# Four or five magnitude products in the windows of steps 8, 16 and 24, and row results in used-up input rows

## The chip, the cores and the metric

The kernel runs on one core of a Trainium2 chip, alone. The metric is the device time of one execution in microseconds (us). TensorE (PE) multiplies matrices, VectorE (DVE) and ScalarE (ACT) work element by element, GpSimd (POOL) does so too, and SyncE (SP) issues nearly all transfers. Each engine takes its instructions in the order in which they were written and waits where a result or a buffer is missing. SP's queue is such an order as well: a transfer that has to wait keeps back every transfer behind it.

## The reference

Two blocks follow each other, on 2048 tokens (L) of 448 channels (D), in float32:

```
mod = silu(c) @ w_mod                                   # six rows: sa, ca, ga, sb, cb, gb
h = layernorm(x) * (1 + ca) + sa
# S4D: K[d, l] = 2 Re sum_n C[d,n] dt[d] exp(A[d,n] dt[d] l), n = 256; A = -exp(log_A_real) + i A_imag
y = irfft(rfft(h, 2L) * rfft(K, 2L))[:L] + h * D_skip   # a causal convolution along the tokens
x = x + ga * y
h = layernorm(x) * (1 + cb) + sb
x = x + gb * (W2 gelu(W1 layernorm(h)^T + b1) + b2)^T   # an MLP across the tokens, 1792 wide
```

## The kernel before

The change touches only the first third, in which the convolution's kernel K is made while the input's own transform is worked off beside it.

K is made in 56 steps (`NHALF`), each for 16 of the 448 channels and half of the 256 n. A step s needs magnitudes and phases. The magnitudes of eight steps (`BATCH`) are made together in a **window** ahead of the steps 0, 8, 16, 24 and so on, because ACT must change its function table between the exponential and the sine. The eight steps behind a window are called its **set**. In a window, place e (0 to 7) takes on ACT the two exponentials of step s + e into a tile `mag` (`st_exp`), while PE makes the exponents of the next step (`st_exponents`). In a step (`st_step`) ACT takes absolute values and sines of the phases that PE made (`st_phase`, in PSUM), POOL multiplies them with the magnitudes to G (two instructions, L737 and L738), DVE to E (four instructions, L739, L740, L742 and L743), and two steps later PE multiplies G and E into kg (`st_kgen`).

Two of the four E instructions need a second magnitude, m2. It is made on POOL by `st_mag2`: a small product w (L712) and a product m of 128x512 (L717). This pair is called a magnitude product here. In the sets of steps 8, 16 and 24, the products of the first two steps are made in the window (e < 2), and that of step s + 2 during step s for the other six. The m2 tiles come from a ring of three (`m2`), the E tiles from a ring of three (`gp_`, tag E).

Beside it run two other lines of work, spread over windows and steps by hand:

- **Rows.** `u_rows(n)`, n from 0 to 31, multiplies a row block of the input `xt` with a table on PE, and DVE scales the result into a tile (L595). Two n make a pair; a pair's result goes to `yu_d` in DRAM from SP. Pair p reads input row block p of the sixteen in `xt`. Its result tile is one of a ring of three (`yt`), except for the pairs 2 to 4, which borrow two E tiles (`yE`). Once steps 12, 13 and 14 are reached, three loads of `w_mod` (L341) overwrite row blocks 0 to 3, 4 to 7 and 8 to 11 of `xt`, to be read by `modulation` in the window of step 16.
- **Columns.** `u_cols(p)` loads `yi` back from `yu_d` (SP, L617), multiplies on PE (`pu`, L627) and adds on DVE (`uo`, L631). The first loads stand in SP's queue behind the window of step 16; the columns fill the steps from 17 on and the window of step 24.
- **Parameter chains.** `chain(q)` prepares, on DVE, the parameters of the next 128 channels; `more` draws some instructions of it at each place. In the windows, its results (A, s, ph, p, xa) are split on POOL into a high and a low part (`hl`: a CAST, L404, and a subtraction, L406) and stored to `pars` in DRAM by SP (L410). Phases (`lph`) and exponents (`lex`) are loaded from there.

All four compute engines have their order written out by hand (a manual schedule); from step 8 on a scheduler orders SP's queue.

Of the kernel before, what the change touches and what calls it, by code (L numbers as in the profile page):

```python
# [11 lines left out]
F32 = mybir.dt.float32  # L12
# [9 lines left out]
L, D, N, F = 2048, 448, 256, 1792  # L22
P = 128
# [3 lines left out]
NI, NJ = 32, 64  # L27
GD = 16
NG = D // GD
NHALF = 2 * NG  # L30
BATCH = 8
# [201 lines left out]
def tile_adaln_s4d_mixer(ctx, tc, i, out):  # L233
# [19 lines left out]
    with ExitStack() as es:  # L253
# [22 lines left out]
        xp = spec.enter_context(tc.tile_pool(name="xp", bufs=1))  # L276
# [28 lines left out]
        xt = xp.tile([P, 16, D], F32, name="xt")  # L305
# [204 lines left out]
        def angle():  # L510

            for a, s, u, xa, ya in tmp.values():
                S.activation(xa, ya, AF.Arctan)
# [52 lines left out]
            T.matmul(pm, wu, means, start=True, stop=True)  # L566
            dve.append(lambda: V.tensor_copy(means, pm))

        yts, wurs, lent = {}, {}, []

        def u_table(R):
            wurs[R] = xp.tile([P, 2, P], F32, tag="wur", name="wur", bufs=3)
# [3 lines left out]
        def u_rows(n):  # L576

            R, g = divmod(n, 4)
            gp, gl = divmod(g, 2)
            if gl == 0:  # L580
                pair = n // 2
                if pair in (2, 4):
                    E = gp_.tile([P, 2, GD, NJ], F32, tag="E", name="yE")
                    rooms = E.rearrange("p a g j -> p (a g j)")[:, 0 : 4 * D].rearrange("p (h g d) -> p h g d", h=2, g=2)
                    lent.extend(rooms[:, h] for h in range(2))
                yts[R, gp] = lent[pair - 2] if 2 <= pair < 5 else xp.tile([P, 2, D], F32, tag="yt", name="yt", bufs=3)
            if g == 0 and R < 6:
                u_table(R + 2)
            pm = pms.tile([P, D], F32, tag="ms", name="pu")
            p = slice(64 * gl, 64 * gl + 64)  # L590
            T.matmul(pm, wurs[R][p, gp], xt[p, 2 * R + gp], start=True, stop=True)  # L591

            def out():
                mean = means[:, gl, 2 * R + gp : 2 * R + gp + 1]
                stt(yts[R, gp][:, gl], pm, mean, mod[1], ALU.add, ALU.mult)  # L595
                if gl:
                    nc.sync.dma_start(
                        yu_d[:, :, :, R, 2 * gp : 2 * gp + 2].rearrange("o k c g d -> (o k c) (g d)"),
                        yts.pop((R, gp)).rearrange("p g d -> p (g d)"),
                    )  # L600

            dve.append(out)
# [36 lines left out]
                u_load(p + 4)  # L639


        mags, m2s, eg, phs = {}, {}, {}, {}
        v32 = lambda t: t.rearrange("p (d i) -> p d i", i=32)

        def rows_of(g, exps):
# [63 lines left out]
        def st_mag2(s):  # L709
            me = v32(mags[s][:, 0])  # L710
            w = wp.tile([P, GD], F32, tag="w", name="w")
            G.tensor_tensor(w[:, :, None], me[:, :, 31:32], me[:, :, 1:2], ALU.mult)  # L712
            if s in (3, 4, 5):
                m2 = v32(wm0.rearrange("p k d -> p (k d)")[:, -512 * (s - 2) :][:, 0:512])
            else:
                m2 = m2p[s >= 32 and s % BATCH > 2].tile([P, GD, 32], F32, tag="m2", name="m2")
            G.tensor_tensor(m2, me, w[:, :, None].to_broadcast([P, GD, 32]), ALU.mult)  # L717
            m2s[s] = m2

        def st_step(s, between):  # L720
            me, mg_, m2 = v32(mags[s][:, 0]), v32(mags[s][:, 1]), m2s.pop(s)
            E = gp_.tile([P, 2, GD, NJ], F32, tag="E", name="E")
            Gt = gp_.tile([P, 2, GD, NI], F32, tag="G", name="G")
# [15 lines left out]
            V.tensor_tensor(E[:, 1, :, 32:64], m2, se, ALU.mult)  # L739
            V.scalar_tensor_tensor(E[:, 1, :, 31::-1], me[:, :, 31::-1], -1.0, se, ALU.mult, ALU.mult)  # L740
            between()
# [350 lines left out]
        def window(s):  # L1092
            if s:
                aside.append(True)
            angle()
            logs(s == 8)
            if s == 8:
                more(10)
                u_scale()
                u_table(0)  # L1100
                u_table(1)

            if s == 0:
                st_exponents(s)
            for e in range(BATCH):
                st_exp(s + e)

                if e + 1 < BATCH:
                    st_exponents(s + e + 1)
                else:  # L1110
                    st_phase(s)
                mellow()
                flush(dve)
                flush(act)
                if s == 8 and e == 0:
                    tt(mod[1], mod[1], mod[2], ALU.mult)
                if s < 32:
                    more(WPACE[s // 8][e])
                if s == 0 and e >= 4:
                    u_stats(e - 4)  # L1120
                if s == 8 and e in (3, 4):
                    modulation(0, e - 3)
                if s == 8 and e == 5:

                    G.tensor_tensor(mod[0], mod[0], mod[2], ALU.mult)
                if s and e < (2 if s <= 32 else 1):
                    st_kgen(s - (2 if s <= 32 else 1) + e)
                elif e == 5 and s < 24:
                    if s == 8:
                        yks[0] = y0.tile([P, 32, DC], F32, tag="yk", name="yk0")  # L1130
                    st_s1(act)

                for k, e0 in ((4, 1), (5, 3), (3, 6)) if s == 16 else ():
                    if e in (e0, e0 + 1):
                        modulation(k, e - e0)

                if s == 8 and e == 0:
                    warm(7)
                if s == 8 and e == 1:
                    u_means()  # L1140
                if s in (8, 16):
                    some(u_rows, rows, ((0, 2, 2, 2, 2, 0, 2, 2) if s == 8 else (2, 2, 2, 2, 2, 0, 1, 1))[e])
                elif s == 24 and e in (0, 2, 4, 6, 7):
                    some(u_cols, cols, 1)

                if s == 0 and e > 1:
                    st_mag2(e - 2)
                elif s and (e < 2 or s >= 32):
                    st_mag2(s + e)
                if s == 0 and e == 3:  # L1150
                    for r in range(4):
                        dsk_copy(r)
            aside.clear()
            if s == 8:
                flush(dve)
            if s >= 24 and st_s1(dve):
                flush(dve)
            if s == 0:

                S.activation(one, one, AF.Sin)  # L1160

        WPACE = [[0, 2, 2, 1, 1, 1, 1, 1], [2, 2, 2, 2, 1, 3, 3, 1], [4] * 7 + [9], [4] * 8]
        pace = [2] * 5 + [3, 4, 4] + [2] * 24
        for s in range(NHALF):
# [13 lines left out]
            if s % BATCH == 0:  # L1180
                (late_window if s > 32 else window)(s)
                if s == 0:
                    gp_ = right("gp", 3)
# [45 lines left out]
                idle(10)  # L1229
            held = s > 32 and s % BATCH == BATCH - 2  # L1230
            free = s > 7 and not st_s1(hold if held and s + 2 < NHALF else dve if s % BATCH == BATCH - 1 else act)
            if s + 2 < 32 and (s + 2) % BATCH > 1 and s + 2 > 5:
                st_mag2(s + 2)

            if 3 < s < 8:
# [146 lines left out]
    with ExitStack() as es:  # L1382
# [169 lines left out]
        for t in range(16):  # L1552
            ss = slice(t * P, (t + 1) * P)
            xt = ru.tile([P, D], F32, tag="x2", name="x2")
# [42 lines left out]
```

## Time and profile before

| | |
|---|---|
| times of the runs shown | 663.41 us median of 3 (663.27 to 668.56) |
| the profiled execution | 663.85 us |
| its span | 662.1 us |
| granted TensorE clock, mean | 0.984 |
| busy: PE, DVE, ACT, POOL | 612.3, 443.0, 439.9, 269.5 us |
| E on DVE, one of four (L740) | 680 ns, 56 times |
| G on POOL, one of two (L737) | 1283 ns, 56 times |
| m on POOL (L717) | 1053 ns, 53 times |
| column result on DVE (L631) | 672 ns, 32 times |
| windows of steps 8, 16, 24 in the span | about 61 to 79, 112 to 131, 161 to 175 us |

A row of a timeline reads: start, duration, engine, line, operation, out<-in, shapes, count; in brackets the idle time of the engine before it and what ended that. SPq is the time in which SP issues a transfer, PEld a weight load of PE. A row of the chain of waits has start, duration and what. In the table of windows, each engine has its busy time in the stretch and the number of instructions.

### The profile page before, as it was taken

What the parts mean: (1) busy time and instruction counts of PE and PEld (TensorE: products, weight loads), DVE (VectorE), ACT (ScalarE), POOL (GpSimd) and SP (SyncE); (2) the same over time, 40 slices, a digit from 0 to 9 for tenths busy, and PEclk for the clock granted to TensorE, in tenths of its full rate; (3) what the DMA queues carried; (4) which work ended last, traced back from release to release, by engine and by line L of the source; (5) the groups of instructions that cost most, each with busy time, mean ns of one, the idle gap of its engine ahead of it and who ended that gap; (6) DMA issues with size and microseconds to landing.
All of it is one profiled execution on the core that took longest, in us unless ns stands there. A gap on an engine that the chain in (4) does not pass through costs nothing.

```text
span 662.1 us, 19161 instructions
## 1 busy us (share of the span) xinstructions
PE 612.3 (92%) x7639; PEld 442.9 (67%) x7639; DVE 443.0 (67%) x853; ACT 439.9 (66%) x828; POOL 269.5 (41%) x351
## 2 busy tenths in 40 slices
PE   1878998999999999999888999999999999999997
PEld 0444555445455565656544577788999999999996
DVE  8989889689894887868655688777422553333331
ACT  5978888899989999999587678885222522222220
POOL 7785597588599788787563000000000000000000
PEclk9998999989999999999999899999999999999999
DMA  6595747598775557576787999946755275555530
GB/s 145 156 219 166 253 143 257 182 248 268 218 247 178 103 166 218 169 215 182 234 274 227 257 247 234 233 112 196 201 160 153 57 209 164 162 160 166 161 106 28
DMA packets 97858, 123.67 MB, mean 187 GB/s; under 512 B 13717, under 2 KB 79801, under 8 KB 97769
## 3 DMA queue, kind: packets, MB, share of 16 engines
q1 hardware_dynamic: 97032, 120.02, 64.2%
q0 software_dynamic: 736, 2.43, 1.5%
q8 instruction: 60, 0.98, 0.7%
q14 instruction: 30, 0.24, 0.1%
HBM read 88.33 MB, written 33.59 MB: 184 GB/s over the span
## 4 chain that ended last, share of the span: by engine, by line
PE 63%; DMA 11%; DVE 9%; ACT 7%; POOL 4%; issue 4%; SPq 3%; ACTq 0%; DVEq 0%; POOLq 0%
PE o L1563 7%; PE o L1565 7%; PE o L1564 7%; PE acc L1400 6%; PE acc L1401 6%; PE acc L1402 6%; PE xe L667 6%; PE kg L764 6%; DMA w<-in_B_w_dram 3%; PE xg L667 3%; DMA xt<-in_A_u_dram 3%; DMA v_d<-vt 3%; PE pu L591 2%; PE vv L895 2%; PE kx L872 2%
## 5 line engine op out<-in xcount | busy, mean ns | idle before, releaser
L218 ACT CAST whi<-w 128x896 fp32r<-128x896 f32 x64 | 59.7, 939 | 138.5 <-PE o L1564 82.7
L227 DVE TENSOR_TENSOR wlo<-w,whi 128x896 fp32r<-128x896 f32 x64 | 68.1, 1086 | 41.4 <-ACT whi L218 35.1
L737 POOL TENSOR_TENSOR G<-mag,gs 128x512 f32<-128x512 f32 x56 | 71.9, 1283 | 36.4 <-ACT gs L733 36.4
L1400 PE MATMUL acc<-h3h,whi 128*128 128x448 f32 x224 | 83.0, 371 | 1.7 <-ACT h3h L1467 0.9
L1401 PE MATMUL acc<-h3l,whi 128*128 128x448 f32 x224 | 81.4, 363 | 0.5 <-DVE h3l L1474 0.3
L1563 PE MATMUL o<-uh,whi 128*128 128x448 f32 x224 | 81.3, 363 | 0.0
L1565 PE MATMUL o<-uh,wlo 128*128 128x448 f32 x224 | 81.2, 362 | 0.0
L1402 PE MATMUL acc<-h3h,wlo 128*128 128x448 f32 x224 | 81.0, 361 | 0.0
L1564 PE MATMUL o<-ul,whi 128*128 128x448 f32 x224 | 80.6, 360 | 0.0
L764 PEld LDWEIGHTS kg<-E,G 128*32 128x32 f32 x3584 | 56.2, 114 | 33.1 <-issue 18.4
L738 POOL TENSOR_TENSOR G<-mag,gs 128x512 f32<-128x512 f32 x56 | 71.9, 1285 | 0.0
L764 PE MATMUL kg<-E,G 128*32 128x64 f32 x3584 | 65.9, 227 | 6.4 <-issue 4.2
L667 PE MATMUL xg<-tab,lph 64*128 64x512 f32 x112 | 62.0, 553 | 6.6 <-DVE E L743 4.3
L1568 DVE TENSOR_TENSOR y<-o,x 128x448 f32<-128x448 f32 x16 | 10.0, 624 | 79.0 <-PE o L1565 79.0
L667 PE MATMUL xe<-tab,lph 64*128 64x512 f32 x112 | 61.9, 553 | 0.3 <-issue 0.2
L717 POOL TENSOR_TENSOR m<-mag,w 128x512 f32<-128x512 f32 x53 | 55.8, 1053 | 4.2
L1400 PEld LDWEIGHTS acc<-h3h,whi 128*128 128x128 f32 x224 | 42.0, 188 | 14.8 <-issue 2.1
L729 ACT ACTIVATE ab<-xe 128x512 f32<-128x512 f32 x56 | 33.9, 604 | 16.3 <-PE xg L667 9.1
L1401 PEld LDWEIGHTS acc<-h3l,whi 128*128 128x128 f32 x224 | 42.0, 187 | 3.8 <-DVE h3l L1474 0.9
L1565 PEld LDWEIGHTS o<-uh,wlo 128*128 128x128 f32 x224 | 42.1, 188 | 3.4
L1402 PEld LDWEIGHTS acc<-h3h,wlo 128*128 128x128 f32 x224 | 42.0, 187 | 3.1
L1564 PEld LDWEIGHTS o<-ul,whi 128*128 128x128 f32 x224 | 41.9, 187 | 3.0
(257 smaller groups left out, 1399.1 us busy)
## 6 DMA issues: line engine op xcount, KB each, us to landing
w<-in_B_w_dram SPq DMA_DIRECT2D x64, 224.0 KB
w<-in_B_w_dram SPq DMA_DIRECT2D x32, 448.0 KB
yi<-yu_d SPq DMA_DIRECT2D x32, 224.0 KB
us_d<-uo SPq DMA_DIRECT2D x16, 448.0 KB
u<-us_d SPq DMA_DIRECT2D x64, 112.0 KB
v_d<-vt SPq DMA_DIRECT2D x32, 224.0 KB
vt<-v_d SPq DMA_DIRECT2D x14, 448.0 KB
yu_d<-yt SPq DMA_DIRECT2D x13, 448.0 KB
```

What stands on the lines that cost most here:

```text
L218: self.nc.scalar.copy(hi, w)
L227: eng.tensor_tensor(lo, w, hi.bitcast(F32), ALU.subtract)
L667: T.matmul(out[k], lhs[r], rhs[r], start=start, stop=stop)
L737: G.tensor_tensor(Gt[:, 1], mg_, v32(sg), ALU.mult)
L738: G.tensor_tensor(Gt[:, 0], mg_, v32(cg_), ALU.mult)
L764: T.matmul(kg[32 * q : 32 * q + 32, m], Gt[:, c, d], E[:, c, d], start=h == 0 and c == 0 and m == 0, stop=h == 1 and c == 1, skip_group_ch ...
L1400: nc.tensor.matmul(acc[f], hi[:, fs], h3h[:, r], start=r == 0, stop=False)
L1401: nc.tensor.matmul(acc[f], hi[:, fs], h3l[:, r], start=False, stop=False)
L1402: nc.tensor.matmul(acc[f], lo[:, fs], h3h[:, r], start=False, stop=r == 15)
L1563: nc.tensor.matmul(o, hi[:, ks], uh[kh][:, k], start=kh == 0 and k == 0, stop=False)
L1564: nc.tensor.matmul(o, hi[:, ks], ul[kh][:, k], start=False, stop=False)
L1565: nc.tensor.matmul(o, lo[:, ks], uh[kh][:, k], start=False, stop=kh == 1 and k == 6)
```

## The change

Three things are changed together.

1. **More products in the windows.** A table `MSET` says how many of a set's magnitude products are made in its window: four for the set of step 8, five for those of steps 16 and 24, where there were two. In the steps two, three and three products are left out, those of the first steps of a set.
2. **Two of them in a tile of E.** At the start of these windows a tile is taken from the E ring (`mE`); its two halves hold the products of the first two steps of the set. The others take the m2 ring as before.
3. **Row results in used-up input rows.** The pairs 2 to 4 no longer borrow E tiles. The pairs 3, 4, 6, 8 and 14 write their results over row blocks of `xt` that were already read (0 and 1, 2 and 3, 4 and 5, 6 and 7, 12 and 13). The other eleven pairs use the `yt` ring.

```diff
-        yts, wurs, lent = {}, {}, []
+        yts, wurs = {}, {}
+        spare = {3: 0, 4: 1, 6: 2, 8: 3, 14: 6}
...
             if gl == 0:
                 pair = n // 2
-                if pair in (2, 4):
-                    E = gp_.tile([P, 2, GD, NJ], F32, tag="E", name="yE")
...
-                yts[R, gp] = lent[pair - 2] if 2 <= pair < 5 else xp.tile([P, 2, D], F32, tag="yt", name="yt", bufs=3)
+                if pair in spare:
+                    yts[R, gp] = xt[:, 2 * spare[pair] : 2 * spare[pair] + 2]
+                else:
+                    yts[R, gp] = xp.tile([P, 2, D], F32, tag="yt", name="yt", bufs=3)
...
-            if s in (3, 4, 5):
+            if s in rooms:
+                m2 = rooms.pop(s)
+            elif s in (3, 4, 5):
...
         def window(s):
...
+            if s in (8, 16, 24):
+
+                E = gp_.tile([P, 2, GD, NJ], F32, tag="E", name="mE")
+                for k in range(2):
+                    rooms[s + k] = E[:, k].rearrange("p g j -> p (g j)")[:, 0:512].rearrange("p (d i) -> p d i", i=32)
...
-                elif s and (e < 2 or s >= 32):
+                elif s and e < (BATCH if s >= 32 else MSET[s // BATCH]):
                     st_mag2(s + e)
...
+        MSET = [0, 4, 5, 5]
...
-            if s + 2 < 32 and (s + 2) % BATCH > 1 and s + 2 > 5:
+            if s + 2 < 32 and (s + 2) % BATCH >= max(2, MSET[s // BATCH]) and s + 2 > 5:
                 st_mag2(s + 2)
```

The order of the instructions on PE and ACT is the same as before. On POOL, in the window of step 16 (the splits of ph, p and xa, the addition ks), before:

```order
L404 CAST hl<-ph 128x256
L784 TENSOR_TENSOR ks<-ks,dsk 128x8
L406 TENSOR_TENSOR hl<-ph,hl 128x256
L404 CAST hl<-p_1199 128x256
L406 TENSOR_TENSOR hl<-p_1199,hl 128x256
L404 CAST hl<-xa 128x256
L406 TENSOR_TENSOR hl<-xa,hl 128x256
```

and now:

```order
L404 CAST hl<-ph 128x256
L712 TENSOR_TENSOR w<-mag 128x16
L719 TENSOR_TENSOR m_2048<-mag,w 128x512
L786 TENSOR_TENSOR ks<-ks,dsk 128x8
L406 TENSOR_TENSOR hl<-ph,hl 128x256
L404 CAST hl<-p_1206 128x256
L712 TENSOR_TENSOR w<-mag 128x16
L719 TENSOR_TENSOR m_2075<-mag,w 128x512
L406 TENSOR_TENSOR hl<-p_1206,hl 128x256
L712 TENSOR_TENSOR w<-mag 128x16
L719 TENSOR_TENSOR m_2094<-mag,w 128x512
L404 CAST hl<-xa 128x256
```

The products of the steps 18, 19 and 20 stand among the splits now; they stood behind the G of the steps 16, 17 and 18.

On SP, in the steps from 11 on (yu_d: a pair's result; xt<-in_w_mod: a w_mod load; lph: phase parameters), before, from the result of pair 6 on:

```order
L597 DMA yu_d<-yt 128x896
L653 DMA lph_141<-pars_58 32x256
L657 DMA lph_141<-pars_58 64x1x256
L341 DMA xt<-in_w_mod_dram 112x4x448
L597 DMA yu_d<-yt 128x896 x2
L653 DMA lph_139<-pars_58 32x256
L657 DMA lph_139<-pars_58 64x1x256
L597 DMA yu_d<-yt 128x896 x2
L341 DMA xt<-in_w_mod_dram 112x4x448
```

and now, from the same pair on:

```order
L597 DMA yu_d<-xt 128x896
L653 DMA lph_141<-pars_58 32x256
L657 DMA lph_141<-pars_58 64x1x256
L597 DMA yu_d<-yt 128x896
L597 DMA yu_d<-xt 128x896
L653 DMA lph_139<-pars_58 32x256
L657 DMA lph_139<-pars_58 64x1x256
L341 DMA xt<-in_w_mod_dram 112x4x448
L597 DMA yu_d<-yt 128x896 x2
L341 DMA xt<-in_w_mod_dram 112x4x448
```

The second w_mod load has moved from ahead of the results of pairs 7 and 8 to behind them, ahead of those of pairs 9 and 10. The first one, not shown, has moved from between the results of pairs 2 and 3 to behind that of pair 5.

More of the change, by code (lines that the diff above doesn't have):

```diff
@@ L581, in u_rows @@
                 pair = n // 2
-                if pair in (2, 4):
-                    E = gp_.tile([P, 2, GD, NJ], F32, tag="E", name="yE")
-                    rooms = E.rearrange("p a g j -> p (a g j)")[:, 0 : 4 * D].rearrange("p (h g d) -> p h g d", h=2, g=2)
-                    lent.extend(rooms[:, h] for h in range(2))
-                yts[R, gp] = lent[pair - 2] if 2 <= pair < 5 else xp.tile([P, 2, D], F32, tag="yt", name="yt", bufs=3)
+                if pair in spare:
+                    yts[R, gp] = xt[:, 2 * spare[pair] : 2 * spare[pair] + 2]
+                else:
+                    yts[R, gp] = xp.tile([P, 2, D], F32, tag="yt", name="yt", bufs=3)
             if g == 0 and R < 6:
@@ L639, in u_cols @@
                 u_load(p + 4)
-        mags, m2s, eg, phs = {}, {}, {}, {}
+        mags, m2s, eg, phs, rooms = {}, {}, {}, {}, {}
         v32 = lambda t: t.rearrange("p (d i) -> p d i", i=32)
```

## The prediction

> **What bounds the kernel now.** The page's list of waits says little about the sets of eight steps, so I read first the chain of waits from 175 to 206 us, which covers the third of the three changed sets (its `by line` sum), and beside it the busy time of each engine in the stretches where the steps run.
>
> ```profile
> by line: POOL G L737 28.8%; POOL G L738 24.1%; issue 17.7%; DMA pars<-hl 9.8%; POOL m L717 5.2%; ACT L696 4.1%; POOL w L712 3.9%; ACT gs L734 2.0%; ACT mag L696 1.9%; ACT xg L735 1.6%; POOL hl L406 1.5%; ACT ks L778 1.0%; POOL hl L404 0.9%;
> ...
> core 0: us, PE busy (x) PEld busy (x) DVE busy (x) ACT busy (x) POOL busy (x), PEclk, DMA share, GB/s
> 144.97:162.90 17.93, 17.70 (x412) 9.63 (x401) 17.93 (x30) 16.81 (x36) 17.31 (x18) 1.00 0.89 272
> 179.00:201.60 22.60, 21.68 (x483) 11.71 (x475) 22.60 (x39) 20.28 (x41) 22.13 (x25) 1.00 0.78 248
> ```
>
> The chain runs through POOL: G and the products m fill it. Taken alone it says that a product less on POOL is a product less in time. The windows below it speak against that: DVE is busy for 17.93 of 17.93 us and for 22.60 of 22.60 us in the second and third set, POOL for 17.31 and 22.13. Both are full. So the next question is what a product costs, and where POOL really keeps somebody waiting.
>
> ```profile
> 97.58 0.26 POOL L712 TENSOR_TENSOR w<-mag 128x16 f32<-128x16 f32 x1
> 97.91 1.05 POOL L717 TENSOR_TENSOR m<-mag,w 128x512 f32<-128x512 f32 x1
> 98.92 1.28 POOL L737 TENSOR_TENSOR G<-mag,gs 128x512 f32<-128x512 f32 x1
> ...
> 201.17 1.29 POOL L737 TENSOR_TENSOR G<-mag,gs 128x512 f32<-128x512 f32 x1
> ...
> 201.36 0.61 ACT L732 ACTIVATE xe<-xe 128x512 f32<-128x512 f32 x1
> 202.49 0.60 ACT L733 ACTIVATE gs<-xg 128x512 f32<-128x512 f32 x1 [0.52 <-POOL G L737]
> ```
>
> A product is its w and its m: from 97.58 to 98.92, so 1.34 us of POOL. The one place where ACT waits for POOL in the third set is step 31: L733 starts at 202.49 when G of step 30 ends (201.17 and 1.29 is 202.46), 0.52 us late. In the steps before it, ACT follows PE and DVE; POOL merely falls behind, and nobody needs its G until two steps later. The second set has no such wait.
>
> In the first set DVE stops once:
>
> ```profile
> 96.04 0.37 SPq L341 DMA_DIRECT2D xt<-in_w_mod_dram  x1
> ...
> 102.15 0.67 DVE L595 SCALAR_TENSOR_TENSOR yt<-pu,means,mod 128x448 f32<-128x448 f32 x1
> 104.32 0.68 DVE L595 SCALAR_TENSOR_TENSOR yt<-pu,means,mod 128x448 f32<-128x448 f32 x1 [1.50 <-DMA yu_d<-yt]
> ...
> 96.50 7.72 DMA yu_d<-yt
> ```
>
> DVE waits 1.50 us, to 104.32, for a buffer of the result ring yt, whose transfer (issued 96.50) took 7.72 us behind a w_mod load issued at 96.04 on the same queue.
>
> **The change, part by part.** All durations are of the profiled execution, which took 663.85 us (span 662.1); the median of the runs shown is 663.41, so 0.44 is taken off at the end. Differences are written with a sign, plus being slower.
>
> *Products out of the steps (2, 3 and 3 of them).* POOL is relieved of 2.7, 4.0 and 4.0 us. DVE, full in sets two and three, keeps the pace: two E products, two more and two uo, as before. What remains is the wait at 202.49. POOL is then ahead by more than the 0.52 us, so ACT goes on to the next table load that much earlier; with the step from 201.36 to its successor at half a microsecond I take **-0.6** (bounds -0.6 and -0.4). What is late next is DVE, which frees the PSUM of the phases.
>
> *Results in input rows.* The ring yt now serves eleven pairs and not thirteen, and pair 10 finds a buffer of pair 5, sent long before: the wait of 1.50 goes, **-1.5**. What comes next: the second w_mod load (L341) has to wait until pairs 6 and 8 have left the rows that it overwrites. It stood ahead of pair 7 on SP, now it stands behind pair 8 and ahead of pair 9, and it will run beside pairs 9 and 10 as it ran beside pair 7. Pair 9 is written at 102.82 (102.15 and 0.67), with 0.7 from the first window (below) 103.5; if its transfer takes 7.72 too, it lands at 111.2. Its buffer goes to pair 12, the first of three at 111.47:
>
> ```profile
> 111.47 1.86 DVE L595 SCALAR_TENSOR_TENSOR yt<-pu,means,mod 128x448 f32<-128x448 f32 x3
> ```
>
> Less 1.5, plus 0.7, that is 110.7: a wait of 0.5 by this count, none if the transfer takes 7 us, more if the third load stretches it. So 0 to +1.1, and I take **+0.4**. The w_mod loads themselves are read by modulations of the second window only, and the lph and lex loads behind them a set later.
>
> *Products into the windows.* Here POOL had gaps, but two things hang on it. In the second window (before step 16):
>
> ```profile
> 124.06 0.40 POOL L404 CAST hl<-ph 128x256 fp32r<-128x256 f32 x1 [1.22 <-DVE ph L419]
> 124.58 0.80 POOL L406 TENSOR_TENSOR hl<-ph,hl 128x256 fp32r<-128x256 f32 x1
> 125.73 0.40 POOL L404 CAST hl<-p 128x256 fp32r<-128x256 f32 x1 [0.35 <-DVE p L425]
> 126.21 0.73 POOL L406 TENSOR_TENSOR hl<-p,hl 128x256 fp32r<-128x256 f32 x1
> 129.19 0.40 POOL L404 CAST hl<-xa 128x256 fp32r<-128x256 f32 x1 [2.25 <-DVE xa L445]
> 129.66 0.72 POOL L406 TENSOR_TENSOR hl<-xa,hl 128x256 fp32r<-128x256 f32 x1
> ...
> 130.41 0.32 SPq L410 DMA_DIRECT2D pars<-hl  x1
> 130.83 0.37 SPq L653 DMA_DIRECT2D lex<-pars  x1
> 131.30 0.50 SPq L657 DMA_DIRECT2D lex<-pars  x1
> 131.99 5.30 SPq L617 DMA_DIRECT2D yi<-yu_d  x8
> ...
> 138.54 0.20 PEld L627 LDWEIGHTS pu<-yi,s 64*64 64x64 f32 x6 [0.39 <-DMA yi<-yu_d]
> ```
>
> The splits of ph, p and xa follow the parameter chain on DVE. The last one ends at 130.38, SP sends it at 130.41, and only behind that and two lex loads may the eight yi loads start (131.99). PE waits for them: the weight load of the first column product stands 0.39 us for yi, at 138.54. So there is no slack from the split of xa to PE, and behind that matmul stand kg of step 16 and the phases of step 18 on. The change puts three products between these splits: 3 x 1.34 = 4.0 us, of which the gaps of 0.35 and 2.25 take up 2.6. That alone makes yi **+1.4** late. The other thing is that DVE and POOL stand in each other's way:
>
> ```profile
> 62.13 0.43 DVE L434 TENSOR_TENSOR xa<-xa,A_C_real 128x256 f32<-128x256 f32 x1
> ...
> 124.83 0.84 DVE L425 TENSOR_TENSOR p<-ph,u 128x256 f32<-128x256 f32 x1
> 126.31 0.91 DVE L434 TENSOR_TENSOR xa<-xa,A_C_real 128x256 f32<-128x256 f32 x1
> 127.45 0.42 DVE L438 SCALAR_TENSOR_TENSOR xa<-xa,A_C_imag 128x256 f32<-128x256 f32 x1
> ```
>
> L434 takes 0.43 us at 62.13 and 0.91 beside POOL's L406 at 126.21; it is done 0.28 after that ends. L425 takes 0.84 beside L406 at 124.58. L438, with POOL idle, 0.42. DVE's operations on SBUF alone seem to wait until POOL's instruction is over. With three products among them, up to ten chain operations take turns with POOL. Upper bound: all serial. DVE's operations from 124.51 to 129.12 are 3.5 us without waiting, POOL's with the products 7.6, together 11.1 from 123.94, which ends at 135.0 and not 130.4: +4.6. Lower bound: +1.4. Since the two single operations were held by 0.4 and 0.5, and some three more will be, not all on the way to xa, I take 1.4 + 1.1 = **+2.5**.
>
> The Trainium skill, "SBUF — State Buffer" (section "SBUF: two separate sides"), calls this an exclusive lock: the first of a GpSimd instruction and a VectorE instruction with two SBUF inputs has the shared ports for its whole length and the other blocks fully. The rows of L434 and L425 agree; by that rule the place would cost near the upper bound, 2.1 us above the value taken, and the sum below would end at 667.3.
>
> In the first window the same happens to DVE, whose chain feeds the rows' results there:
>
> ```profile
> 75.09 1.14 POOL L1125 TENSOR_TENSOR mod<-mod,mod 128x448 f32<-128x448 f32 x1
> 76.19 0.79 POOL L574 TENSOR_TENSOR wur<-wu,rs 128x256 f32<-128x256 f32 x1
> ...
> 75.86 0.66 DVE L457 TENSOR_TENSOR s<-xa,ya 128x256 f32<-128x256 f32 x1
> 76.55 0.72 DVE L459 TENSOR_TENSOR ya<-ya,xa 128x256 f32<-128x256 f32 x1
> 79.29 0.42 DVE L465 TENSOR_TENSOR ya<-ya,xa 128x256 f32<-128x256 f32 x1
> 79.83 1.27 DVE L595 SCALAR_TENSOR_TENSOR yE<-pu,means,mod 128x448 f32<-128x448 f32 x2
> ```
>
> L457 and L459 are held by L1125 and L574, L465 is not, since POOL is done at 76.98. Two products more put POOL's end 2.7 us later, at 79.7, so L461 to L468 meet it: 0 (they slip between) to +1.2 (L465 waits out L1125); **+0.7**. PE waits for that L595. The ks addition, now behind product 10, is 1.3 us later too, and PE's y waits for it; that is counted inside the same 0.7.
>
> In the third window the chain works on half the elements; product 26 can hold one operation for the 1.05 us of an m, so 0 to +1.0; **+0.3**, since most chain operations lie elsewhere. Products 27 and 28 lie behind a split that waits for a transfer anyway; what they push is G of step 24, and the relieved steps make that good. The order of the E buffers costs nothing: the two products in E are read by DVE itself before E is written again.
>
> The sum: 0.7 - 1.5 + 0.4 + 2.5 + 0.3 - 0.6 = **+1.8 us**; 665.65 profiled, **665.2** as a median. With all lower ends -0.7 (662.7), with all upper ends +6.0 (669.4): this case's own range.
>
> **The rivals.**
>
> 1. *POOL sets the pace, as the chain has it.* Then the third set gives 3 x 1.34 = 4.0: 659.4; if all sets do, 8 x 1.34 = 10.7: 652.7. For it: the shares of L737 and L738. Against: DVE's 22.60 of 22.60. Chance 0.12 (0.02 for all sets).
>
> 2. *The windows swallow it.* POOL's products fit its gaps, the yi loads are served faster when late, and both waits go: -1.5 - 0.6, so 661.3. For it: products beside E operations, which read PSUM, cost DVE nothing. Against: the weight load that stood for yi. Chance 0.14.
>
> 3. *Slower: PE at half clock.* Place: the start of set 16. These are the 64 matmuls kg of a step there, and of the next step:
>
> ```profile
> 140.06 1.93 PE L764 MATMUL kg<-E,G 128*32 128x64 f32 x64
> 144.05 1.10 PE L764 MATMUL kg<-E,G 128*32 128x64 f32 x64
> ```
>
> Ahead of the row at 140.06 PE stood still, 1.04 us for DVE and then for yi:
>
> ```profile
> 136.88 0.47 PE L667 MATMUL xg<-tab,lph 64*128 64x512 f32 x1 [1.04 <-DVE E L743]
> ```
>
> If yi is late by the upper bound, PE stands some 4 us and steps 17 to 19 may all run like that: kg +0.8 and the column products about +1.2 in each, two steps more than now, +4.0. With the turns at their upper end (+2.1) that is 665.2 + 6.1 = 671.3. It decides if PE's stand exceeds what it had at 137. Chance 0.06. The Trainium skill, "TensorE: Matmul & The Clock Gate" ("What's actually happening"), has the clock halve after an idle window of some 3.4 us; here the slow kg follows a stand of 1.04 us, so the trace is the stricter one.
>
> The order of the instructions shows that the change does what it says; that it does not is no rival.
>
> **How the numbers follow.** The forecast has 0.68. The range 660.0 to 669.0 holds nearly all of it, the second rival and a part of the first. A measurement of this kernel tells about 1% (6.6 us) from no change: faster than 656.8 is only the first rival's far end, 0.02; slower than 670.0 is the third rival but for its milder outcomes, 0.05; the rest, 0.93, is within.
>
> **What would show it.** Right: no wait of L595 for yu_d near 104; no wait of ACT for POOL at step 31; L434 to L445 in the second window at 0.7 to 1.4 us each; the yi loads issued about 2 us later against step 16's own start, and PE standing longer for yi; the E operations of sets two and three still without a gap. Wrong: if DVE shows gaps in the sets and steps shorten to 3.1 us, DVE was not the bound; if L438 stays at 0.42 beside a product, the turn-taking was not it.

## The result, and the profile after

| | before | after |
|---|---|---|
| median of the runs | 664.53 us of 14 (662.07 to 669.44) | 669.36 us of 14 (666.13 to 670.92 but for one disturbed run of 829.64, which the ratio leaves out) |
| ratio | | 1.0067, 95% interval 1.0045 to 1.0088 |
| the profiled execution, its span | 663.85, 662.1 us | 669.98, 668.2 us |
| granted TensorE clock in it | 0.984 | 0.982 |
| busy PE, DVE, ACT, POOL | 612.3, 443.0, 439.9, 269.5 us | 615.0, 447.8, 440.1, 271.1 us |

The change makes the kernel slower by 0.67%, 4.5 us on the median of before. That is within 1%, as forecast, and the sign is right; the predicted 665.2 is 4.2 us short of this median, which lies 0.4 us above the range. But the kernel before has its median at 664.53 here and not at the 663.41 that the prediction started from; the ratio on 663.41 gives 667.9, which is 2.7 us above the forecast and inside the range. From here on the lines are those of the changed kernel: G is L739 and L740, m L719, the sines L734, E L741 to L745, kg L766, the rest as before.

**Where the 6.1 us between the two profiled executions arise.** ACT loads a function table at fixed places of the program, so the starts of these loads cut both traces into the same stretches. The timeline of ACT, first before, then after:

```profile
80.08 1.28 ACT L732 ACT_TABLE_LOAD   x1
112.35 1.28 ACT L501 ACT_TABLE_LOAD   x1
132.07 1.28 ACT L732 ACT_TABLE_LOAD   x1
```

```profile
80.72 1.28 ACT L734 ACT_TABLE_LOAD   x1
113.58 1.28 ACT L501 ACT_TABLE_LOAD   x1
137.44 1.28 ACT L734 ACT_TABLE_LOAD   x1
```

The set of step 8 (first row to second) went from 32.27 to 32.86 us, the window of step 16 (second to third) from 19.72 to 23.86. By the same rows elsewhere the window of step 8 is +0.77, the set of step 16 -0.14, the window of step 24 +0.33, its set -0.06, and everything behind +0.64. So the window of step 16 carries 4.1 of the 6.1 us.

**The second window.** The timeline of DVE, POOL and ACT there, in the changed kernel:

```profile
128.02 1.22 DVE L425 TENSOR_TENSOR p<-ph,u 128x256 f32<-128x256 f32 x1
131.02 1.23 DVE L438 SCALAR_TENSOR_TENSOR xa<-xa,A_C_imag 128x256 f32<-128x256 f32 x1
132.28 0.84 DVE L440 SCALAR_TENSOR_TENSOR xa<-ph,xa 128x256 f32<-128x256 f32 x1
133.48 1.15 DVE L445 TENSOR_TENSOR xa<-xa,u 128x256 f32<-128x256 f32 x1
...
130.91 1.05 POOL L719 TENSOR_TENSOR m<-mag,w 128x512 f32<-128x512 f32 x1
133.30 1.05 POOL L719 TENSOR_TENSOR m<-mag,w 128x512 f32<-128x512 f32 x1
135.18 0.72 POOL L406 TENSOR_TENSOR hl<-xa,hl 128x256 fp32r<-128x256 f32 x1
...
135.93 0.31 ACT L451 ACTIVATE xa<-A_C_real 128x128 f32<-128x128 f32 x1 [2.07 <-POOL hl L406]
...
137.42 5.28 SPq L617 DMA_DIRECT2D yi<-yu_d  x8
```

L425, L438 and L445 took 0.84, 0.42 and 0.43 us before (L425 was held by a split there); beside a product they take 1.15 to 1.23. From L423 to the end of L445 the chain needs 6.94 us (127.69 to 134.63) where it needed 4.61. The split of xa ends at 135.90 and not 130.38, and what starts then is ACT's L451, after a stand of 2.07 us for POOL: the first operation of the next chain, which writes the buffer xa and must wait until the split has read it. Before, it had no such stand:

```profile
130.53 0.35 ACT L451 ACTIVATE xa<-A_C_real 128x128 f32<-128x128 f32 x1
```

The sines of step 16 stand behind it on ACT. The yi loads are late too (137.42, before 131.99), but by no more than step 16 itself: against its table load they are issued 0.02 us ahead, before 0.08 us. PE's weight load stands 0.59 us for yi (at 144.10) and not 0.39. That yi would be late by 2 us against step 16 and PE stand longer for it, as the forecast had it, did not come.

**Half-clock stretches.** In the first window DVE is held as well, and PE then does something that the sum did not hold. The timelines of DVE, PE and ACT, changed kernel:

```profile
77.58 1.14 DVE L461 TENSOR_SCALAR s<-s 128x256 f32<-128x256 f32 x1
...
81.81 1.70 PE L591 MATMUL pu<-xt,wur 64*128 64x448 f32 x2 [1.78 <-DVE xt L595]
83.45 2.21 PE L679 MATMUL kg<-ones 128*128 128x256 bf16 x10
...
86.85 0.60 ACT L731 ACTIVATE ab<-xe 128x512 f32<-128x512 f32 x1 [2.75 <-PE xg L667]
```

and those of PE and ACT before:

```profile
80.57 1.02 PE L591 MATMUL pu<-xt,wur 64*128 64x448 f32 x2 [1.16 <-DVE yE L595]
81.52 1.26 PE L679 MATMUL kg<-ones 128*128 128x256 bf16 x10
...
83.97 0.60 ACT L729 ACTIVATE ab<-xe 128x512 f32<-128x512 f32 x1 [0.50 <-PE xg L667]
```

PE stands 1.78 us for L595 (1.16 before), and behind it its work is slow: ten idle matmuls (L679, matmuls on constants that only keep PE busy) take 2.21 us, not 1.26, and ACT waits 2.75 us for the phases of step 9, not 0.50. The busy times in stretches of 3.41 us show the clock (the column behind POOL's), after:

```profile
78.59:82.00 3.41, 1.63 (x12) 0.81 (x8) 3.34 (x6) 3.08 (x5) 1.70 (x2) 1.00 0.30 106
82.00:85.41 3.41, 3.41 (x12) 1.50 (x11) 3.13 (x7) 2.10 (x5) 2.23 (x2) 0.50 0.43 151
112.72:116.14 3.42, 2.09 (x67) 1.39 (x65) 3.00 (x6) 3.37 (x7) 1.80 (x2) 1.00 0.92 331
116.14:119.55 3.41, 3.14 (x67) 2.48 (x69) 2.08 (x5) 3.21 (x6) 1.91 (x4) 0.50 0.26 88
119.55:122.96 3.41, 3.41 (x74) 2.11 (x74) 1.53 (x3) 1.08 (x2) 1.11 (x3) 0.50 0.44 167
```

and before:

```profile
77.33:80.74 3.41, 2.25 (x15) 1.20 (x14) 3.34 (x6) 3.08 (x6) 0.00 (x0) 1.00 0.94 232
80.74:84.15 3.41, 3.41 (x40) 1.85 (x44) 3.41 (x7) 2.90 (x6) 1.61 (x2) 1.00 0.85 322
114.87:118.28 3.41, 3.41 (x71) 2.52 (x70) 1.61 (x4) 3.25 (x6) 1.87 (x4) 0.50 0.15 41
118.28:121.70 3.42, 3.42 (x82) 1.57 (x80) 1.57 (x4) 1.97 (x4) 2.01 (x4) 1.00 0.55 215
```

Behind the first window PE runs 3.4 us at half clock where it ran at full clock before; at the start of the second window there are two such stretches in a row where there was one. By this a stretch of half clock costs PE 1.71 us of work, half of its 3.41.

**What came as forecast.** The wait of 1.50 us for yu_d near 104 is gone; one of 0.41 us has come for pair 12 (+0.4 was the term). The timeline of DVE and, for step 31, of ACT:

```profile
113.20 1.87 DVE L595 SCALAR_TENSOR_TENSOR yt<-pu,means,mod 128x448 f32<-128x448 f32 x3 [0.41 <-DMA yu_d<-yt]
...
207.99 0.60 ACT L735 ACTIVATE gs<-xg 128x512 f32<-128x512 f32 x1
```

The last row is the sine of step 31 that waited 0.52 us for G of step 30; it has no wait now. In the chain of waits of the third set (180.5 to 211.5 us), G and m on POOL are no longer among the large shares:

```profile
by line: PE pu L627 23.9%; PE xe L667 20.5%; PE kg L766 13.3%; issue 5.1%; PE xg L667 4.5%; ACT L696 4.1%; DVE uo L631 4.1%; ACT gs L735 3.9%; PE y L804 3.7%; ACT gs L732 3.5%; ACT gs L736 3.3%; ACT ab L731 2.6%; DVE E L745 2.0%; ACT mag L6
```

The busy times of the second and third set:

```profile
150.34:168.13 17.79, 17.55 (x405) 9.60 (x397) 17.79 (x30) 16.72 (x36) 16.35 (x17) 1.00 0.89 273
184.80:207.10 22.30, 21.41 (x458) 11.23 (x457) 22.17 (x38) 19.74 (x40) 18.60 (x18) 1.00 0.82 261
```

DVE is still full (22.17 of 22.30 us in the third set), and POOL is relieved, 18.60 us busy there instead of 22.13 of 22.60. The set did not become shorter for it (28.90 us, before 28.96).

### The profile page after: what moved, and what is told of

Its sections match the earlier page's. It is cut to its first block, busy times and chain, and to the rows that moved or that the text cites. A ratio compares the mean times of both kernels' runs of the same rounds, so it can differ in the third digit from the quotient of the medians.

```text
span 668.2 us, 19149 instructions
## 1 busy us (share of the span) xinstructions
PE 615.0 (92%) x7639; PEld 443.5 (66%) x7639; DVE 447.8 (67%) x853; ACT 440.1 (66%) x828; POOL 271.1 (41%) x351
## 4 chain that ended last, share of the span: by engine, by line
PE 70%; DVE 9%; DMA 8%; ACT 6%; issue 3%; POOL 3%; SPq 1%; ACTq 0%; DVEq 0%; POOLq 0%
PE xe L667 8%; PE kg L766 7%; PE o L1572 7%; PE o L1571 7%; PE o L1573 7%; PE acc L1408 6%; PE acc L1409 6%; PE acc L1410 6%; PE xg L667 4%; DMA w<-in_B_w_dram 3%; PE pu L627 3%; PE vv L897 2%; PE pu L591 2%; PE kx L874 2%; PE y L804 2%
## 5 line engine op out<-in xcount | busy, mean ns | idle before, releaser
L739 POOL TENSOR_TENSOR G<-mag,gs 128x512 f32<-128x512 f32 x56 | 72.0, 1285 | 45.5 <-ACT gs L735 45.4
L766 PEld LDWEIGHTS kg<-E,G 128*32 128x32 f32 x3584 | 56.0, 114 | 32.5 <-issue 21.5
L740 POOL TENSOR_TENSOR G<-mag,gs 128x512 f32<-128x512 f32 x56 | 71.9, 1284 | 0.0
L766 PE MATMUL kg<-E,G 128*32 128x64 f32 x3584 | 65.5, 227 | 5.8 <-issue 4.3
L719 POOL TENSOR_TENSOR m<-mag,w 128x512 f32<-128x512 f32 x47 | 49.7, 1057 | 3.7
L731 ACT ACTIVATE ab<-xe 128x512 f32<-128x512 f32 x56 | 33.8, 603 | 18.7 <-PE xg L667 10.8
L1571 PEld LDWEIGHTS o<-uh,whi 128*128 128x128 f32 x224 | 42.0, 188 | 3.4
```

The source lines that it names most:

```text
L739: G.tensor_tensor(Gt[:, 1], mg_, v32(sg), ALU.mult)
L740: G.tensor_tensor(Gt[:, 0], mg_, v32(cg_), ALU.mult)
L766: T.matmul(kg[32 * q : 32 * q + 32, m], Gt[:, c, d], E[:, c, d], start=h == 0 and c == 0 and m == 0, stop=h == 1 and c == 1, skip_group_ch ...
L1571: nc.tensor.matmul(o, hi[:, ks], uh[kh][:, k], start=kh == 0 and k == 0, stop=False)
```

## The experiments

In all of them the results of five pairs stay in used-up input rows. The table has the lengths of the first window (W8), its set (S8), the second window (W16) and its set (S16) in each profiled execution, cut at ACT's table loads as above (W8 from the second load of its window, W16 from the first); in brackets the half-clock stretches in them (of 3.4 us, by the granted clock in stretches of 0.25 us). The ratio is to the kernel before, with its 95% interval.

| | W8 | S8 | W16 | S16 | ratio |
|---|---|---|---|---|---|
| before | 17.19 | 32.27 (0) | 19.72 (1) | 29.00 (1) | 1 |
| after | 17.96 | 32.86 (1) | 23.86 (2) | 28.86 (1) | 1.0067 (1.0045-1.0088) |
| e1_rows | 17.89 | 30.86 (0) | 18.51 (0) | 28.93 (0) | 1.0011 (0.9987-1.0035) |
| e2_set8 | 17.47 | 32.65 (1) | 18.53 (0) | 28.97 (0) | 1.0039 (1.0021-1.0057) |
| e3_set16 | 17.20 | 32.45 (1) | 20.69 (0) | 29.15 (2) | 1.0008 (0.9983-1.0034) |
| e4_set24 | 17.87 | 30.89 (0) | 18.51 (0) | 28.94 (1) | 1.0013 (0.9990-1.0037) |
| f1_warm8 | 17.76 | 31.34 (0) | 21.62 (1) | 29.26 (2) | 1.0080 (1.0051-1.0108) |
| f5_warm3 | 19.50 (1) | 31.15 (0) | 20.86 (0) | 29.97 (1) | 1.0035 (1.0008-1.0063) |
| f2_xa2 | 18.76 (1) | 33.23 (1) | 20.29 (1) | 31.70 (2) | 1.0062 (1.0038-1.0087) |
| f3_late16 | 18.42 (1) | 33.78 (1) | 18.51 (0) | 31.27 (2) | 1.0037 (1.0016-1.0059) |
| h1_set8_warm | 17.52 | 31.95 (0) | 21.12 (1) | 28.93 (0) | 1.0050 (1.0023-1.0077) |
| h2_early | 18.64 | 30.63 (0) | 20.74 (0) | 29.46 (2) | 1.0073 (1.0052-1.0093) |
| h3_no16 | 18.40 (1) | 33.29 (1) | 18.53 (0) | 28.95 (1) | 1.0022 (0.9998-1.0045) |
| h4_24_warm | 17.34 | 31.04 (0) | 18.70 (0) | 28.95 (0) | 0.9990 (0.9973-1.0007) |

### One part at a time

e1_rows leaves the products as before; the others make more products in one window only. In e1_rows:

```diff
-            if s in (8, 16, 24):
+            if s in ():
...
-        MSET = [0, 4, 5, 5]
+        MSET = [0, 2, 2, 2]
```

e2_set8 has `(8,)` and `[0, 4, 2, 2]`, e3_set16 `(16,)` and `[0, 2, 5, 2]`, e4_set24 `(24,)` and `[0, 2, 2, 5]`.

> Only the row results in used input rows; two products in every window as before, no tile mE. Clock theory (the loss is half-clock stretches of PE after longer stands, in the first window and at the start of the second, plus the second window's chain, which holds ACT): the yu_d wait of 1.5 us goes and PE stands less in set 8, so -1.1 to -1.5 us against before (ratio 0.998), unless the new wait of 0.4 for pair 12 alone is what doubles the half-clock stretch at the start of the second window, then about +0.5. Forecast's terms: -1.5 + 0.4 = -1.1 us. A rival, that the w_mod loads behind later pairs are what costs: +1 us or more, with ACT or PE waiting for wm tiles in the second window.

> Row results in input rows and four products in the window of step 8 alone. Clock theory: PE stands about 1.8 us for L595 near 80, runs at half clock for 3.4 us, L731 of step 9 comes some 2.9 us later than before; of that the yu_d wait gives 1.5 back: +1.4 us, and up to +3.3 if the stretch at the start of the second window doubles too. Forecast's terms: +0.7 - 1.5 + 0.4 = -0.4 us.

> Row results in input rows and five products in the window of step 16 alone. Theory that the split of xa holds ACT's L451: DVE's chain L423 to L445 takes 6.9 us and not 4.6, ACT stands about 2 us for POOL, step 16 starts 2.3 us later; with the rows' -1.1 that is +1.2 us (3 if a half-clock stretch is added). Forecast's terms: +2.5 - 1.1 - 0.6 = +0.8 us, by PE standing longer for yi, ACT not standing. The two differ in who stands, not in the time.

> Row results in input rows and five products in the window of step 24 alone. Clock theory and forecast's terms: +0.3 on the rows' -1.1, so -0.8 us; with ACT's wait at step 31 gone -1.4 us by the forecast. A rival, that five products in any window of this size hold ACT as in the second: +1 us or more.

The rows alone shorten S8 by 1.41 us (32.27 to 30.86), the 1.5 of the forecast. The time doesn't show it: 1.0011, with an interval that reaches from -0.9 to +2.3 us. W8 is 0.70 us longer in e1_rows than before, although it has no more products, but e3_set16, which makes the same products up to that point, has 17.20: traces differ by so much, and the 0.77 of the changed kernel can't be told from that.

e2_set8 is slower by 2.6 us, as the clock theory had it (+1.4 to +3.3; the forecast's terms gave -0.4), and its S8 is 1.8 us longer than that of e1_rows, with one half-clock stretch. In e3_set16, W16 is 2.18 us longer than in e1_rows without any such stretch in either, and ACT's L451 stands for POOL:

```profile
130.65 0.31 ACT L451 ACTIVATE xa<-A_C_real 128x128 f32<-128x128 f32 x1 [2.07 <-POOL hl L406]
...
122.75 1.23 DVE L425 TENSOR_TENSOR p<-ph,u 128x256 f32<-128x256 f32 x1
125.74 1.22 DVE L438 SCALAR_TENSOR_TENSOR xa<-xa,A_C_imag 128x256 f32<-128x256 f32 x1
```

So 2.2 us is what three products among the splits cost, and the one who stands is ACT, as the first theory had it. The time of e3_set16 (1.0008) doesn't tell it from nothing. For set 24, e4_set24 has 14.21 us in the window (e1_rows 14.02) and 28.82 in the set (29.45). With two products there as well, e3_set16 has 15.17 and 28.61, so neither difference is shown to come from the products; nor is there one in time.

The same part was also undone from the whole, with `(8, 24)` and `[0, 4, 2, 5]`:

> The changed kernel with the set of step 16 alone as before (two products in its window, no tile mE there). If the parts add: rows with set 8 measured 1.0039 and set 24 nothing, so 1.004, the window's sines 2.2 us earlier than with the five products. If sets 8 and 16 add more together than apart (a later second window meeting a longer half-clock stretch): 1.003 to 1.004 here all the same, and the whole of 1.0067 is then set 16's 2.2 us beside a second stretch. Rival, that set 16 costs nothing on the path, as its part alone measured (1.0008): 1.0067.

h3_no16 measured 1.0022: the products of set 16 cost 0.45%, 3.0 us, of the 0.67% (by the two intervals 0.9 to 5.1 us). The rival (1.0067) is out. The four parts, rows +0.0011 and over the rows +0.0028, -0.0003 and +0.0002, add up to 1.0038, less than 1.0067. Undone from the whole, set 16 weighs more than alone; the intervals, 1.2 to 1.7 us to both sides, don't settle how much of that is real.

### What hangs on the split of xa

f2_xa2 gives the last chain's first buffer another place, so that ACT need not wait for the split:

```diff
+            xr = t if q == 3 else xa
-            for to, src in (xa, cr), (ya, ci):
+            for to, src in (xr, cr), (ya, ci):
...
-            V.reciprocal(xa, s)
+            V.reciprocal(xr, s)
```

(and likewise in the three further operations of this chain that use the buffer).

> The changed kernel with the magnitude of A_C_real of the last chain (L451) and its reciprocal in the tile t, so that ACT need not wait for POOL's split of xa. Theory that ACT's stand delays step 16: the stand of 2.07 us goes, E of step 16 starts about 1.5 us earlier against the changed kernel, ratio 1.0045. Forecast's mechanism, that yi binds: PE then stands some 2 us for yi behind step 16, the time stays as the changed kernel's (1.0067, at most 0.5 us less).

ACT's stand is gone, and W16 is 1.33 us shorter than in f1_warm8, which has as many half-clock stretches there (20.29 against 21.62). S16 gives it all back, 31.70 and not 29. PE's timeline in f2_xa2 shows why:

```profile
139.68 0.47 PE L668 MATMUL xg<-tab,lph 64*128 64x512 f32 x1 [1.02 <-ACT gs L733]
142.69 2.47 PE L628 MATMUL pu<-yi,s 64*64 64x448 f32 x8 [1.86 <-DMA yi<-yu_d]
```

The column products now wait 1.86 us for yi. The time (1.0062) is that of the changed kernel, as the second theory said. Two things hang on the same split, ACT's L451 and the yi loads; taking one away uncovers the other.

f3_late16 issues the three products behind the split:

```diff
-                elif s and e < (BATCH if s >= 32 else MSET[s // BATCH]):
+                elif s and e < (BATCH if s >= 32 else 2 if s == 16 else MSET[s // BATCH]):
...
+            if s == 16:
+                for e in range(2, MSET[2]):
+                    st_mag2(s + e)
```

> The changed kernel with products 18 to 20 issued behind the split of xa, at the end of the window of step 16. Turn-taking as the cause of the second window's length: L423 to L445 takes 4.6 us again, ACT does not stand for POOL, step 16 starts 2.3 us earlier; the products then meet the last chain and come ahead of G of step 16, which gives up to 1.0 back: -1.3 to -2.3 us against the changed kernel, ratio 1.003 to 1.005. Rival, that the second window's length comes from the clock alone: no change (1.0067).

W16 falls to 18.51 us, the length without the products. S16 takes 2.3 us more. There the products meet the last chain, on DVE:

```profile
133.36 1.07 DVE L461 TENSOR_SCALAR s<-s 128x128 f32<-128x128 f32 x1
135.99 1.24 DVE L470 SCALAR_TENSOR_TENSOR s<-t,s 128x128 f32<-128x128 f32 x1
137.15 0.67 DVE L741 TENSOR_TENSOR E<-mE,xe 128x512 f32<-128x512 f32 x1
```

L461 takes 1.07 us (0.22 in the changed kernel at 137.08), L470 1.24 (0.29). E of step 16 starts 3.85 us behind the sines' table load (133.30), and not 1.91 as before (132.07 to 133.98). The products hold whichever chain they meet. The ratio (1.0037) is the one expected, but not for the reason given: what W16 gains by the move, S16 loses. The changed kernel's profile had two half-clock stretches in W16 and this one has none; by the lengths of the profiles (below) that alone may be 3.1 us, and W16 and S16 together are 2.9 us shorter (49.78 against 52.72). That the move itself is worth something is not shown.

h2_early issues each window's products ahead of that round's chain operations:

```diff
+                if 0 < s < 32 and e < MSET[s // BATCH]:
+                    st_mag2(s + e)
                 if s < 32:
                     more(WPACE[s // 8][e])
...
-                elif s and e < (BATCH if s >= 32 else MSET[s // BATCH]):
+                elif s >= 32:
                     st_mag2(s + e)
```

> The changed kernel with each window's products issued ahead of that round's chain operations, so that product 18 falls into POOL's idle time before the cast of ph. Turn-taking theory: one product less among L423 to L445, the split of xa 1.3 us earlier against the window's own start, 1.3 us less in time than the changed kernel: ratio 1.0047. If only the number of products in the window counts, wherever they stand: 1.0067 as the changed kernel.

The 1.3 us less did not come: W16 is 20.74 us, as in e3_set16, and the time 1.0073. POOL was late at that place and had no gap left, and the three products held L419 (product 18), L430 (19) and L438 (20), where they hold L425, L438 and L445 in the changed kernel:

```profile
122.21 1.15 DVE L419 TENSOR_TENSOR ph<-ph,u 128x256 f32<-128x256 f32 x1
124.53 1.14 DVE L430 TENSOR_SCALAR xa<-xa 128x256 f32<-128x256 f32 x1
127.23 1.22 DVE L438 SCALAR_TENSOR_TENSOR xa<-xa,A_C_imag 128x256 f32<-128x256 f32 x1
129.68 0.43 DVE L445 TENSOR_TENSOR xa<-xa,u 128x256 f32<-128x256 f32 x1
```

From L415 to the end of L445 the chain takes 8.61 us (121.50 to 130.11), in the changed kernel 8.59 (126.04 to 134.63). Here the number of products beside the chain counted, not their place.

### The clock

f1_warm8 fills PE's stand in the first window with ten idle matmuls, f5_warm3 two more stands:

```diff
+                if s == 8 and e == 7:
+                    warm(10)
...
-                    warm(10)
+                    warm(26 if s == 17 else 10)
...
+            if s == 15:
+                warm(8)
```

f1_warm8 has the first of these three edits alone.

> The changed kernel with ten idle matmuls (1.3 us) on PE ahead of the last two row products of the window of step 8, where PE stands 1.78 us for L595. Clock theory: PE keeps its full clock behind 82 us, L731 of step 9 comes near 85.1 and not 86.85, about 1.75 us less than the changed kernel, so +2.7 us against before (ratio 1.004). Rival, that the stand and not the clock is what costs: no change against the changed kernel (1.0067), or +0.3 us more.

> The changed kernel with idle matmuls on PE in three stands: ten as in f1, eight (1.0 us) ahead of the y products behind step 15, sixteen more (2.0 us) behind the phases of step 17. Clock theory: two half-clock stretches less on the path, the third is beside a wait for DVE anyway: 3.4 us less than the changed kernel, about +1.0 us against before (ratio 1.0015), with a mean granted clock near 0.987. Rival, that the stands cost and not the clock: as the changed kernel (1.0067) or slower.

In both, PE keeps its full clock behind the first window, and S8 is 31.34 and 31.15 us against 32.86. PE's timeline in f1_warm8 shows the row products and the next ten idle matmuls at full speed:

```profile
81.21 1.26 PE L679 MATMUL kg<-ones 128*128 128x256 bf16 x10
82.41 2.00 PE L591 MATMUL pu<-xt,wur 64*128 64x448 f32 x4
84.34 1.26 PE L679 MATMUL kg<-ones 128*128 128x256 bf16 x10
```

f1_warm8 nevertheless measured 1.0080, no gain over the changed kernel; its profile has half-clock stretches elsewhere (one at 59.75, one in W16, two in S16, two at 217). f5_warm3 came to 1.0035, 2.1 us less than the changed kernel, of the 3.4 expected; their intervals overlap.

h1_set8_warm is e2_set8 with the first of the three edits, h4_24_warm is e4_set24 with the first (seven matmuls) and the third:

> Row results in input rows and four products in the window of step 8 alone, with ten idle matmuls (1.3 us) ahead of the window's last two row products, where PE stood 1.8 us. Clock theory: no half-clock stretch behind 82 us, set 8 (from its sines' table load to the second window's first) 1.4 us shorter than in the kernel before where it was 0.4 longer without the idle matmuls; 1.7 us less in time than that kernel's 1.0039, so 1.0013. Rival, that the stand itself costs: 1.0039 again.

> A candidate for a version better than both: row results in input rows, five products in the window of step 24 alone, seven idle matmuls in the first window's stand and eight ahead of the y products behind step 15. Clock theory: the part without idle matmuls measured 1.0013 at 5.8 half-clock stretches a run; one less in two of three runs is 1 us: 0.9995 to 1.000, and with the rows' 1.4 us that shows up at 112 us, down to 0.998. Rival, that idle matmuls only shift the stands: 1.0013 or slower.

h1_set8_warm has no half-clock stretch in S8, which is 31.95 us, 0.7 less than in e2_set8 and not 1.8 less. Its time is no better (1.0050 against 1.0039), and its profile has a stretch at the start of W16 instead. So that one fill is worth 1.7 us of time isn't shown by either run; in the lengths of S8 it is plain. h4_24_warm has the lowest time of all, 0.9990; its interval reaches to 1.0007, so it isn't told from the kernel before, and no version here beats it beyond doubt.

**All profiles together.** S8 without a half-clock stretch lasts 30.6 to 32.0 us in seven traces of the new row code, with one 32.5 to 33.8 in six, by the means 31.12 and 33.04: 1.9 us. The products themselves seem to make little difference to S8 (h2_early, with them and without a stretch, 30.63; e3_set16, without them and with one, 32.45). Whether a stretch comes goes with PE's stand for L595 at the end of W8. In the ten kernels without idle matmuls there, before included, the four with a stand of 0.69 to 1.17 us (e4_set24, e1_rows, before, h2_early) have no stretch in S8, and the six with 1.34 to 2.73 us (e3_set16, e2_set8, after, f2_xa2, h3_no16, f3_late16) have one. This division was found in the traces afterwards; no run tested it.

W16 is 18.5 to 18.7 us with two products and no stretch (five traces), 20.7 to 20.9 with five (three traces), and 23.86 with five and two stretches. The products cost 2.2 us, the two stretches of that one trace 3.1. With a single one W16 is 0.9 us longer in f1_warm8 (21.62, five products) and 2.6 in h1_set8_warm (21.12, two products), so what a stretch costs there is known only roughly. S16 is 28.9 to 29.2 with none, one or two in the first six rows of the table: there they cost next to nothing. f1_warm8 and h2_early have 29.3 and 29.5 with two; f5_warm3, at 29.97, has sixteen more idle matmuls in S16.

The granted clock that is on record for every execution gives a price that does not hang on single profiles. (1 - clock) times the span, divided by 1.71 us, is the number of half-clock stretches of an execution, an estimate over the whole span. In the 84 undisturbed executions of the kernel before, the time rises by 1.1 us for each stretch more (standard error 0.13, correlation 0.68). f1_warm8 has 8.1 stretches by this count, the changed kernel 7.2: the idle matmuls took away the stretch in S8, and the number did not fall. In h1_set8_warm it did, 5.5 against 6.1 in e2_set8, without a gain in time.

## Why the prediction was right or wrong

**Right: no gain in the sets.** DVE stayed full, POOL left the chain of waits, step 31 lost its wait, and the third set's length stayed. With that the first rival, POOL setting the pace (4.0 us less in the third set), is out; the second, a gain of 2.1 us, is out by the sign. The forecast's -0.6 for step 31 is not shown: it was 0.06 between the two kernels, and e3_set16 and h1_set8_warm, whose third set is as before, have no wait of ACT for POOL in it and are as short (28.61 and 28.52 us) as e4_set24.

**Right: the rows.** -1.5 was the term, -1.41 the length measured in e1_rows; pair 12's new wait +0.4, measured 0.41 in the changed kernel (e1_rows does not have it).

**Right in size, half right in mechanism: the second window.** The term was +2.5 (1.4 to 4.6), measured 2.2 by turn-taking. The path was only half of it: I had yi as the one thing behind the split of xa. In the changed kernel it is ACT's L451, which the order of the instructions showed waiting for POOL and which had hardly any slack in the kernel before either (L451 at 130.53, the split's end at 130.38). f2_xa2 shows that PE waits 1.9 us for yi once L451 is free. As both are late by the same split, the sum was not hurt. The Trainium skill, "SBUF — State Buffer" (section "SBUF: two separate sides"), also counts a VectorE operation in a two-port mode among those that lock. L461 (1.14 us beside a product, 0.28 before) and L430 (1.14 in h2_early, 0.28 before) have one input and were held too; whether they run in such a mode no trace shows. The sum by full turns (4.6) was still twice too high, since five of the ten chain operations (L423, L430, L434, L436, L443) got through between POOL's instructions.

**Wrong: the first window's +0.7.** This step failed. As a delay it was well sized: PE stands 1.78 us for L595, 0.93 in e1_rows, 1.16 before. But I let it end there. Behind the longer stand PE runs a stretch at half clock (in the traces of all six kernels with a stand of 1.34 us or more, in none of the four with 1.17 or less), and with it S8 is 1.9 us longer; in the changed kernel's trace it ate the whole gain of the rows. Of the six kernels with these products and no idle matmuls, five have it; of the four without the products, e3_set16 alone, so the products make it more frequent and are not needed for it.

**Wrong: the third rival's place.** The mechanism (PE at half clock after standing) was the right one, with 0.06 of chance. I put it at the start of step 16, where the kernel before had a slow kg that was easy to see, and priced it at +4.0. There it costs almost nothing (S16 29.00 with one, 28.93 without): in the changed kernel's stretch at 143.45 ACT is busy for 3.38 of 3.41 us, in the one at 82.00 for 2.10. It costs time in S8 and at the start of the second window, where PE is waited for; in the second window the kernel before had one stretch and the changed one has two. By the count from the granted clock, an execution of the kernel before has 5.1 half-clock stretches (mean clock 0.987, 84 executions); e1_rows has 5.8, the changed kernel 7.2 (0.9815, 13 executions) and h4_24_warm 4.3.

**The sum again.** The forecast's +1.8 held -1.5 + 0.4 for the rows and 2.5 for the second window, found as -1.4, 0.4 and 2.2: +1.2. The smaller terms are below what single profiles tell. The changed kernel has 2.1 stretches more than the one before; at the 1.1 us that a stretch goes with in the kernel before these are 2.3 us, together 3.5, and at 1.9 us, if all lie on the path, 4.0, together 5.2; 4.5 was measured. So the stretches are of the size of what was missing. That taking one away gains its price in time is not shown: f1_warm8 and h1_set8_warm, meant to show it, did not.

## What to carry to other kernels

Work that is moved into another engine's idle time isn't free while a chain of small operations runs beside it on an engine that takes turns with it, here DVE with POOL: count how many operations it will meet, not how long the gaps are, and look for everything behind the end of that chain, a buffer that is used again included. Where PE stands longer, look at the granted clock of the 3.4 us behind, and price it where PE is waited for. Filling a stand with idle matmuls moved the stretch and didn't make the kernel faster beyond doubt. A gain of 1 to 2 us is no more than the times differ from execution to execution, in part with the number of half-clock stretches (standard deviation 1.9 us for the kernel before), so lengths between fixed marks of several traces tell more than the total.

## What the runs showed of the hardware

The half-clock stretches start on a fixed grid. Read in steps of 0.04 us, they begin at 47.87, 82.00, 116.16, 143.45 and 218.54 in the changed kernel: distances of 34.13, 34.16, 27.29 and 75.09 us, which are 10, 10, 8 and 22 times 3.413. In the thirteen other traces they last 3.4 us or twice that, too, and the grid lies elsewhere in each execution. The Trainium skill, "TensorE: Matmul & The Clock Gate" ("What's actually happening"), has a free-running window of 3413 ns; the traces agree to the hundredth. It names an idle window as what lowers the clock; here a window in which PE was busy for half of the time is enough. The windows ahead of a stretch and the stretch, in h3_no16, and in e1_rows, where none follows:

```profile
80.70:84.11 3.41, 1.36 (x6) 0.67 (x7) 3.38 (x7) 3.38 (x6) 0.58 (x1) 1.00 0.43 149
84.11:87.52 3.41, 3.41 (x20) 1.55 (x18) 3.09 (x6) 0.35 (x1) 1.93 (x2) 0.52 0.54 189
```

```profile
79.29:82.70 3.41, 2.48 (x15) 1.13 (x12) 3.38 (x8) 3.19 (x5) 0.00 (x0) 1.00 0.26 83
82.70:86.11 3.41, 3.41 (x85) 2.42 (x83) 2.84 (x6) 3.13 (x7) 2.99 (x4) 1.00 0.57 188
```

Busy for 1.36 of 3.41 us brought the stretch, 2.48 did not. From 76 to 145 us in the traces of before, after and the four single parts, windows of the grid at full clock with PE busy for under 2.1 us were followed by a stretch in six of eight cases, those between 2.1 and 2.4 in three of six, and none with more. Further on, a window between 208 and 219 us brings one in five of these traces although the profile has PE busy for 3.28 to 3.41 us of it. So busy time alone doesn't decide; what else does stays open.
